# Two-MLP in-projections: 42 matmuls by seven half-depth products where four tiles took 48, with the third token block kept plain

## The chip, the core and the metric

One core of a Trainium2 chip runs the kernel. The metric is device time in microseconds of one execution. The core has five engines that run side by side and meet through semaphores: TensorE (PE, matmuls; its weight loads have a row of their own, PEld), VectorE (DVE), ScalarE (ACT), GpSimd (POOL) and SyncE (SP), whose queue issues nearly all transfers here.

## What is computed

An attention over pooled queries, then a softplus MLP, then a gated MLP behind an RMS normalisation, all in float32:

```python
q_pool = q.reshape(B, H, S // 2, 2, D).mean(axis=3)              # B 2, H 8, S 1152, D 64
scores = scale * np.matmul(q_pool, k.transpose(0, 1, 3, 2))
attn = softmax(scores)                                           # over the 1152 keys
x = (attn @ v) as 1152 tokens x 512
h = x @ moe_w_in                                                 # 512 x 2048
x = softplus(h) @ moe_w_out                                      # 2048 x 512
xn = x / sqrt(mean(x * x) + 1e-6) * rms_g
g, val = xn @ w_gate, xn @ w_val                                 # 512 x 1536 each
out = (g * sigmoid(g) * val) @ w_out                             # 1536 x 512
```

## The kernel before

Every activation lies transposed, features on the 128 partitions and tokens along the columns. The 1152 tokens are three blocks of N = 384 columns. A float32 product is made of three matmuls in the round format: an operand is split into a high half and the rest (hi, lo), and `terms` (lines 643 to 646) adds hi x hi, hi x lo and lo x hi in one PSUM bank.

The attention comes first: 8 pairs of heads (`pb`), each of 5 steps (`x`); in a step `qk` (L476) makes scores, `softmax` takes the maximum on VectorE (L490) and the exponential on ScalarE (L492), `flip` (L511) transposes, `av` (L536) multiplies by v. While it runs, `prep` loads and splits the next pair's operands, `shift` and `split` scale a finished pair and split it into the halves `X[t]` of the token blocks, and `decode` brings the first weight tiles in.

Weights lie in memory as 64-bit numbers. `decode(n)` loads a tile of 128 x 512 into `raw` (L268), scales one word on ScalarE (L316), shifts the other on VectorE (L321), joins them (L324 and L326) and splits the result into hi (copy, L257 or L259) and lo (subtraction, L262). A tile has a place of its own, `slots`.

First MLP: for each block t and each of J1 = 16 tiles j, `m1_h` calls `project` (12 matmuls over KC = 4 chunks of the depth 512), takes the softplus (L666) and splits it (`halve`: L257 or L259, L262); `m1_out` calls `expand` (12 matmuls into the four `out` banks). The loop runs over 48 (t, j), with `m1_h` two ahead. Second MLP: for each block and each of J2 = 12 tiles, `m2_in` projects with the gate and the value tile, takes silu (L773), multiplies (L775), splits; `m2_out` expands. Between them `norm_sum`, `norm_rows`, `norm_turn` and `norm` normalise a block and split it into halves again (L759, then L257, L259, L262).

The program doesn't write down an order for the engines. Each step is entered with the engines that may take it and an estimated duration; `Plan.order` and `Plan.run` lay the steps out by due time and write them out in that order. TensorE's steps keep the order in which they were entered. Which engine takes a copy or a subtraction is thus the planner's choice.

## Time and profile before

| | |
|---|---|
| timed runs | 687.08, 687.18, 687.88 us; median 687.18 |
| span of the profiled execution, first to last instruction | 684.7 us |
| the median above that span | 2.5 us |
| TensorE busy | 675.8 us, 99% of the span |
| VectorE, ScalarE, GpSimd busy | 433.1, 333.3, 112.5 us |
| granted TensorE clock, mean | 0.997 of 2.4 GHz |

The page of the profile gives each engine's busy time, the span in slices, and the chain of work that ended last. The views of the trace give groups of equal instructions with their mean duration, the waits, and the instructions of a stretch in order of time. Busy time of TensorE counts two matmuls that are in flight as one stretch, so that a matmul's own duration is longer than the distance to the next; how fast TensorE goes is read from that distance.

### The profile page before, as it was taken

The page shows a single profiled execution, that of the slowest core. Times are in us where ns is not written, and L with a number is a line of the kernel's source. Part 1 is how long each engine was busy: PE and PEld are TensorE (multiplying, and loading weights), DVE is VectorE, ACT ScalarE, POOL GpSimd, SP SyncE. Part 2 cuts the span into 40 slices and gives each one's busy share as a digit, 9 for nine tenths or more (in the row PEclk, how much of TensorE's full clock was granted, in tenths as well). Part 3 has the DMA queues.
Part 4 walks back from the last instruction along what each step waited for, and adds up shares of the span by engine and source line. Part 5 has one row for each costly group of instructions (what it writes and reads, how often), then busy time and mean ns, then how long its engine had stood idle before and what let it go on. Part 6 is the DMA issues. An engine that isn't in the chain of part 4 may idle for free.

```text
span 684.7 us, 12439 instructions
## 1 busy us (share of the span) xinstructions
PE 675.8 (99%) x5067; PEld 654.4 (96%) x5067; DVE 433.1 (63%) x756; ACT 333.3 (49%) x613; POOL 112.5 (16%) x128
## 2 busy tenths in 40 slices
PE   8999999999999999999999999999999999999997
PEld 7998989898898989999999999999999999999997
DVE  8876787787787779998324468888775412231222
ACT  4887888768888886663212333464531300010001
POOL 0551544426332222000000000011221000000000
PEclk9999999999999999999999999999999999999999
DMA  7543433244321234554000023342540100010001
GB/s 203 170 130 90 127 99 94 74 113 124 101 84 63 81 115 164 187 190 147 0 1 1 32 91 113 134 154 95 183 156 30 47 0 1 1 47 0 1 1 46
DMA packets 20854, 59.77 MB, mean 87 GB/s; under 512 B 3839, under 2 KB 6206, under 8 KB 20798
## 3 DMA queue, kind: packets, MB, share of 16 engines
q1 hardware_dynamic: 20286, 58.63, 27.1%
q8 instruction: 39, 0.64, 0.4%
q10 hardware_dynamic: 512, 0.36, 0.2%
q14 instruction: 17, 0.14, 0.1%
HBM read 56.59 MB, written 2.39 MB: 86 GB/s over the span
## 4 chain that ended last, share of the span: by engine, by line
PE 97%; DVE 1%; DMA 1%; ACT 0%; issue 0%; ACTq 0%; DVEq 0%
PE s L644 16%; PE s L645 16%; PE s L646 16%; PE s L476 12%; PE t L536 11%; PE t L511 10%; PE t L646 5%; PE t L645 5%; PE t L644 5%; PE t L816 1%; DMA kr<-in_kT_dram 1%; ACT pt L257 0%; DVE pt L259 0%; PE t L840 0%; PE s L714 0%; DVE kk L262 0%
## 5 line engine op out<-in xcount | busy, mean ns | idle before, releaser
L644 PE MATMUL s<-x,w 128*128 128x384 f32 x348 | 117.3, 337 | 0.0
L646 PE MATMUL s<-x,w 128*128 128x384 f32 x348 | 116.7, 335 | 0.0
L645 PE MATMUL s<-x,w 128*128 128x384 f32 x348 | 116.7, 335 | 0.0
L490 DVE TENSOR_REDUCE nm<-s 128x1 f32<-128x1152 f32 x72 | 97.7, 1357 | 25.4 <-PE s L476 23.9
L492 ACT ACTIVATE p<-s,nm 128x1152 f32<-128x1152 f32 x72 | 88.3, 1226 | 14.4 <-DVE nm L490 12.9
L773 ACT ACTIVATE g<-s 128x384 f32<-128x384 f32 x36 | 17.7, 492 | 143.0 <-PE s L646 142.9
L257 ACT COPY pt<-t 128x512 f32<-128x512 f32 (+2 forms) x138 | 71.2, 528 | 32.6 <-PE t L511 24.0
L511 PE MATMUL t<-ident,p 128*128 128x128 f32 x576 | 83.5, 278 | 2.5 <-DVE pt L259 1.4
L645 PE MATMUL s<-gl,w 128*128 128x384 f32 x243 | 81.6, 336 | 0.0
L644 PE MATMUL s<-gh,w 128*128 128x384 f32 x243 | 81.6, 336 | 0.0
L646 PE MATMUL s<-gh,w 128*128 128x384 f32 x243 | 81.5, 335 | 0.0
L536 PE MATMUL t<-pt,v 128*64 128x128 f32 (+1 forms) x1440 | 80.1, 265 | 0.0
L511 PEld LDWEIGHTS t<-ident,p 128*128 128x128 f32 x576 | 65.0, 140 | 14.0 <-issue 4.5
L536 PEld LDWEIGHTS t<-pt,v 128*64 128x64 f32 x1440 | 71.3, 137 | 7.2 <-issue 7.0
L644 PEld LDWEIGHTS s<-x,w 128*128 128x128 f32 x348 | 65.4, 188 | 0.2 <-issue 0.2
L645 PEld LDWEIGHTS s<-x,w 128*128 128x128 f32 x348 | 65.4, 188 | 0.0
L646 PEld LDWEIGHTS s<-x,w 128*128 128x128 f32 x348 | 65.4, 188 | 0.0
L262 DVE TENSOR_TENSOR gl<-g,gh 128x384 fp32r<-128x384 f32 x83 | 47.3, 570 | 8.9 <-ACT gh L257 6.8
L316 ACT ACTIVATE t<-raw 128x512 f32<-128x512 f32 x68 | 44.8, 670 | 15.7 <-DVE w L262 13.6
L326 DVE SCALAR_TENSOR_TENSOR t<-t,t 128x512 int32<-128x512 int32 x68 | 47.5, 699 | 1.2
L666 ACT ACTIVATE g<-s 128x384 f32<-128x384 f32 x36 | 17.7, 492 | 62.5 <-PE s L646 58.9
L259 DVE CAST gh<-g 128x384 fp32r<-128x384 f32 x56 | 20.2, 360 | 43.6 <-PE t L646 39.5
(149 smaller groups left out, 1200.9 us busy)
## 6 DMA issues: line engine op xcount, KB each, us to landing
raw<-in_w_dram SPq DMA_DIRECT2D x16, 512.0 KB, 3.7
raw<-in_w1o_dram SPq DMA_DIRECT2D x16, 512.0 KB, 3.4
qr<-in_qT_dram SPq DMA_DIRECT2D x28, 288.0 KB, 4.1
raw<-in_wg_dram SPq DMA_DIRECT2D x12, 512.0 KB, 3.5
raw<-in_wv_dram SPq DMA_DIRECT2D x12, 512.0 KB, 3.8
raw<-in_w2o_dram SPq DMA_DIRECT2D x12, 512.0 KB, 3.5
v<-in_v_dram SPq DMA_DIRECT2D x16, 288.0 KB, 3.3
kr<-in_kT_dram SPq DMA_DIRECT2D x7, 576.0 KB, 4.1
```

The lines of the kernel that those rows point to most:

```text
L257: nc.scalar.copy(out, in_)
L262: engines[e].tensor_tensor(out=out, in0=in0, in1=in1, op=o)
L316: o = op([("ACT", 0.68)], lambda e: nc.scalar.activation(out=t0(), in_=word(1).bitcast(F32), scale=2.0 ** -112, **(dict(func=AF.Prelu, alp ...
L326: op([dve(DM)], lambda e: nc.vector.scalar_tensor_tensor(out=t0().bitcast(I32), in0=t0().bitcast(I32), scalar=3, in1=t1(), op0=ALU.logical ...
L476: nc.tensor.matmul(sc()[:, c, :N], lhsT=q()[:, cut], rhs=k()[:, c * N:(c + 1) * N], start=(i == 0), stop=(i == len(todo) - 1))
L490: u["mx"] = op([dve(S, psum=True)], lambda e: nc.vector.tensor_reduce(out=nm(), in_=sc()[:, :, :N], axis=AX.XY, op=ALU.max, negate=True), ...
L492: o = op([("ACT", 1.42)], lambda e: nc.scalar.activation(out=pr(), in_=sc()[:, :, :N], func=AF.Exp, bias=nm(), accum_out=s["den"]()[:, col ...
L511: nc.tensor.transpose(t()[:, i * P:(i + 1) * P], pr[:, c * P:(c + 1) * P], ident)
L536: nc.tensor.matmul(t()[h * D:h * D + D, :n], lhsT=s["v"][h]()[:, c, :], rhs=rhs, start=(c == 0), stop=(c == CK - 1))
L644: nc.tensor.matmul(out, lhsT=w[:, 0, cols], rhs=hi, start=start, stop=False)
L645: nc.tensor.matmul(out, lhsT=w[:, 0, cols], rhs=lo, start=False, stop=False)
L646: nc.tensor.matmul(out, lhsT=w[:, 1, cols], rhs=hi, start=False, stop=stop)
```

## The change

The in-projections of two weight tiles against two token blocks, four tiles of 12 matmuls, are now made from seven products of half the depth (6 matmuls each: two chunks by three terms). The scheme is Winograd's form of Strassen's: with the tiles' depth halves as rows and the token blocks as columns, four mixtures of the weights (`mix`, lines 414 to 417 of the new kernel) and four differences of the tokens (`Tokens.begin` and `end`: t1 to t4) stand for one product less in eight. In the first MLP tiles 2J and 2J + 1 make a pair and blocks 1 and 2 the columns; in the second MLP the gate and the value tile J make a pair and blocks 0 and 1 the columns. The remaining block (0 in the first, 2 in the second) is projected by plain products (`one_by_one`).

`seven` gives the order p1, p5, p2, p6, p7, p3, p4 on three PSUM banks a, b and f. A result that two tiles share is not added by an instruction of its own: `forward` copies a bank into the next (p1 from a to b, p6 from b to f) or into SBUF (`sp`, p5), and the next product adds into the filled bank with `start` false. The two tiles of the first block leave as they are, the other two are added to `sp` (`added`).

Block 0 of the first MLP is expanded inside the loop of 8 passes; the softplus of blocks 1 and 2 is kept whole (`kept`) and expanded afterwards, 16 tiles each (`first_last`, `step`). The second MLP's loop of 12 passes fills in the last five steps of block 2, the plain tiles of block 2 and the expansions of block 0; blocks 1 and 2 are expanded at the end, 12 tiles each.

`decode` takes two tiles at a time and works in place in the loaded room. The weights' halves, the tokens' halves, the kept tiles and the rooms lie in five areas of SBUF (`AREAS`, in columns of four bytes): `Plan.alloc` gives a place, `free` ends its life, and whoever gets it next waits for all users of the last owner. The attention stays as it is but for the split of its result: `arrived` splits block 0 as it comes, and makes the differences of blocks 1 and 2.

```diff
+AREAS = {"KF": 11330, "KR": 15360, "MR": 8760, "LR": 13632, "LF": 4608}
...
+    def alloc(self, cols, areas, end=0):
+        best = None
+        for rank, name in enumerate(areas.split()):
+            size, region = self.areas[name]
+            mine = [h for h in self.held if h[0] == name]
+            edges = {e for h in mine for e in h[1:3]} | {0, size}
+            for at in sorted(edges if end >= 0 else {e - cols for e in edges}):
...
+                over = [h for h in mine if h[1] < at + cols and at < h[2]]
+                if at < 0 or at + cols > size or any(h[3].live for h in over):
+                    continue
+                key = (rank, end * at) if end else (max([h[4] for h in over], default=0), rank, at)
+                if best is None or key < best[0]:
...
+        for b in self.placed:
+            for o in b.ops:
+                for p in b.prior:
+                    for u in p.users:
+                        o.deps.update(u.ops)
...
+    def halve(hi, lo, x, hp, lp, xp, a, z, at=0):
+        n = z - a
+        i, j = a - at, z - at
+        op([dve(n, True), act(n)], lambda e: copy(e, hi()[:, i:j], x()[:, a:z]), r=[(x, p) for p in xp], w=[(hi, p) for p in hp])
+        op([dve(n), pool(n)], lambda e: tt(e, lo()[:, i:j], x()[:, a:z], hi()[:, i:j], ALU.subtract),
+           r=[(hi, p) for p in hp] + [(x, p) for p in xp], w=[(lo, p) for p in lp])
...
-    def decode(n):
-        src, j = pieces[n]
-        b = view = place(n)
-        weights[src, j] = (b, view)
-        raw = ring("k", "raw", [P, 2 * DM], I32, 2)
...
+    def decode(srcs, combine, phase, fs, rs):
+        b = Halves(rs)
+        s = Halves(rs) if combine else None
+        room = plan.alloc(2 * W, fs)
...
+        cuts = ((0, 1), (1, 2)) if phase == "exp" else ((0, 2),)
...
+            op([dve(n, True)], lambda e, x0=x0, x1=x1: nc.vector.tensor_scalar(
+                out=word(0, x0, x1), in0=word(0, x0, x1), scalar1=29, scalar2=None, op0=ALU.logical_shift_right), w=w0)
...
+            mix(0, (1, 2), (1, 0), ALU.subtract, [first, second])
+            mix(1, (1, 3), (1, 2), ALU.add, [second])
+            mix(2, (1, 3), (0, 0), ALU.add, [second, (room, (0, 0))])
+            mix(3, (1, 1), (0, 2), ALU.subtract, [first])
...
+                op([act(n)], lambda e, w=w, t=t, x0=x0, x1=x1: copy(
+                    e, each(t.hi, x0, x1), word(w, x0, x1).bitcast(F32)), r=rp, w=hp)
+                op([pool(n)] if phase == "exp" else [dve(n), pool(n)], lambda e, w=w, t=t, x0=x0, x1=x1: tt(
+                    e, each(t.lo, x0, x1), word(w, x0, x1).bitcast(F32), each(t.hi, x0, x1), ALU.subtract), r=rp + hp, w=lp)
+        plan.free(room)
...
+        def sub(self, out, x, y, kks):
+            out, x, y = self.of(out), self.of(x), self.of(y)
+            a, z = kks[0] * N, (kks[-1] + 1) * N
+            parts = [(k, i) for k in kks for i in range(2)]
+            op([dve(z - a)], lambda e: tt(e, out()[:, a:z], x()[:, a:z], y()[:, a:z], ALU.subtract),
+               r=[(b, p) for b in (x, y) for p in parts], w=[(out, p) for p in parts])
+        def begin(self, kks):
+            n, m = self.two
+            self.sub("t1", (0, m), (0, n), kks)
+            self.halves("b11", (0, n), kks)
+        def end(self, kks):
+            n, m = self.two
+            self.sub("t2", (1, m), "t1", kks)
+            self.halves("t1", "t1", kks)
+            self.sub("t4", (1, n), "t2", kks)
+            self.halves("b21", (1, n), kks)
+            self.halves("t2", "t2", kks)
+            self.sub("t3", (0, m), (1, m), kks)
+            if 1 in kks:
+                plan.free(self.of((0, m)))
+            self.halves("t3", "t3", kks)
+            self.halves("b22", (1, m), kks)
+            self.halves("t4", "t4", kks)
...
+    def arrived(pb):
+        b, k = divmod(pb, H // 2)
+        if b == 0:
+            X1.split_alone(k)
+        elif k == 1:
+            X1.begin([0, 1])
+        elif k > 1:
+            X1.end([k - 2])
...
-    def project(bank, src, j, x):
-            for k in range(KC):
-                terms(view(), w(), slice(k * P, (k + 1) * P), xh()[:, k, :], xl()[:, k, :], k == 0, k == KC - 1)
...
+    def product(bank, w, x, start, seeded=False, stop=True):
+            out = bank()[:, :N]
+            for k in range(2):
+                for i, (a, b) in enumerate(((w.hi, x.hi), (w.hi, x.lo), (w.lo, x.hi))):
+                    nc.tensor.matmul(out, lhsT=a(k), rhs=b(k), start=start and k + i == 0, stop=stop and k + i == 3,
+                                     skip_group_check=seeded)
+        op([("PE", 6 * MM)], go, r=w.deps + x.deps, w=[(bank, None)])
+    def forward(out, o, bank, sbuf):
+        op([act(N, False), dve(N, psum=True)], lambda e: copy(e, out()[:, :N] if not sbuf else out(), bank()[:, :N]),
+           r=[(bank, None)], w=[(out, o)])
+    def added(out, bank, sp):
+        op([dve(N, psum=True)], lambda e: nc.vector.tensor_tensor(out=out(), in0=sp(), in1=bank()[:, :N], op=ALU.add),
+           r=[(bank, None), (sp, None)], w=[(out, None)])
+    def seven(row, col, X, a, b, f, done):
+        (s0, j0), (s1, j1) = row
+        sp = ring("k", "sp", [P, N])
+        def p1():
+            product(a, plain(s0, j0, 0), X.get("b11"), True)
+            forward(b, None, a, False)
+        def p5():
+            product(f, mixed(s0, j0, 1), X.get("t1"), True)
+            forward(sp, None, f, True)
+        def p2():
+            product(a, plain(s0, j0, 1), X.get("b21"), False, True)
+            done("11", a)
+        def p6():
+            product(b, mixed(s0, j0, 2), X.get("t2"), False, True)
+            forward(f, None, b, False)
+        def p7():
+            product(b, mixed(s0, j0, 0), X.get("t3"), False, True)
+            done("22", b, sp)
+        def p3():
+            product(f, mixed(s0, j0, 3), X.get("b22"), False, True)
+            done("12", f, sp)
+        def p4():
+            product(b, plain(s1, j1, 1), X.get("t4"), False, True)
+            done("21", b)
+        return p1, p5, p2, p6, p7, p3, p4
...
+    def one_by_one(bank, src, j, X):
+        for half in range(2):
+            product(bank, plain(src, j, half), X.single(half), half == 0, stop=half == 1)
...
-    for i in range(n1):
-        t, j = divmod(i, J1)
-        if i + 2 < n1:
-            m1_h(i + 2)
-        m1_out(i)
...
+    n1 = J1 // 2
+    later = {0: [(first_pair, 3), (first_out, 3)], 1: [(first_pair, 4), (first_out, 4)], 2: [(first_out, 5)],
+             3: [(first_pair, 5), (first_out, 6)], 4: [(first_pair, 6)], 5: [(first_pair, 7)], 6: [(first_out, 7)]}
+    for J in range(n1):
+        j = 2 * J
+        p1, p5, p2, p6, p7, p3, p4 = seven((("w1", j), ("w1", j + 1)), None, X1, ab, bb, fb, m1_done(J))
+        expand("w1o", j, kept.pop((0, j)), Y)
+        p1()
+        p5()
+        if J + 1 < n1:
+            m1_alone(j + 2, nb)
+        p2()
+        p6()
+        expand("w1o", j + 1, kept.pop((0, j + 1)), Y)
+        p7()
+        p3()
+        drop("w1", j, 2)
+        if J + 1 < n1:
+            m1_alone(j + 3, nb)
+        if J + 2 == n1:
+            X1.free_alone()
+        p4()
+        drop("w1", j, 0)
+        for make, n in later.get(J, ()):
+            make(n, "soft", FS, RS)
+    X1.free_two()
+    X2 = Tokens(2, (0, 1), FS, RS, RS)
+    evict(Y, 0)
...
+    for j in range(J1):
+        first_last(1, j, X)
+        if j in (0, 6):
+            second_pair(j // 6)
+        if j == 2:
+            norm_sum(0)
+        if j == 5:
+            norm_rows(0, Y[3])
+        if j == 8:
+            norm(0, Y[3])
+        if j == 10:
+            second_out(0)
+    evict(X, 1)
...
+    def step(j):
+        first_last(2, j, Y)
+        if j % 2:
+            drop("w1o", j, 0)
+        if j == 0:
+            norm_sum(1)
+        if j == 5:
+            norm_rows(1, nb)
+        if j == 7:
+            norm(1, nb)
+            X2.begin([0, 1])
+            X2.end([0, 1])
+        if j == 9:
+            second_pair(2)
+        if j == J1 - 1:
+            kept_free()
+            evict(Y, 2)
+            norm_sum(2)
...
+    begin = 11
+    fill = {J: [lambda j=begin + 3 * J + i: step(j) for i in range(3 - J)] for J in range(2)}
+    fill[2] = [lambda: (second_first(0), norm_rows(2, nb)), lambda: second_first(1)]
+    for J in range(3, J2):
+        fill[J] = [lambda j=j, w=w: alone(j, w) for j in {3: (0,), 4: (1, 2), 5: (3, 4)}.get(J, (J - 1,)) for w in range(2)]
+        fill[J].insert(0 if J == 3 else len(fill[J]), lambda j=J - 1: second_first(j))
+    for j in range(begin):
+        step(j)
...
+    for J in range(J2):
+        p1, p5, p2, p6, p7, p3, p4 = seven((("wg", J), ("wv", J)), None, X2, ab, bb, fb, m2_done(J))
+        todo = iter(fill[J])
+        def filler(*counts):
+            if len(fill[J]) in counts:
+                next(todo)()
+        p1()
+        p5()
+        filler(3, 5)
+        p2()
+        filler(5)
+        p6()
+        filler(2, 3, 5)
+        p7()
+        filler(5)
+        p3()
+        drop("wg", J, 2)
+        filler(2, 3, 5)
+        p4()
+        if J == 2:
+            norm(2, nb)
+        for make, n in more.get(J, ()):
+            make(n)
+    X2.free_two()
+    kept_halves("2")
+    for which, bank in enumerate((nb, ab)):
+        alone(J2 - 1, which, bank)
+    second_first(J2 - 1)
+    store(Y, 0)
```

TensorE in the first MLP, one in-projection tile of before (`s_3413` is its bank, `x0` the token block, `w18` the tile):

```order
L644 MATMUL s_3413<-x0_1169,w18_3732 128x384
L645 MATMUL s_3413<-x0_1169,w18_3732 128x384
L646 MATMUL s_3413<-x0_1169,w18_3732 128x384
L644 MATMUL s_3413<-x0_1169,w18_3732 128x384
L645 MATMUL s_3413<-x0_1169,w18_3732 128x384
L646 MATMUL s_3413<-x0_1169,w18_3732 128x384
L644 MATMUL s_3413<-x0_1169,w18_3732 128x384
L645 MATMUL s_3413<-x0_1169,w18_3732 128x384
L646 MATMUL s_3413<-x0_1169,w18_3732 128x384
L644 MATMUL s_3413<-x0_1169,w18_3732 128x384
L645 MATMUL s_3413<-x0_1169,w18_3732 128x384
L646 MATMUL s_3413<-x0_1169,w18_3732 128x384
```

And of the new kernel, the in-projection part of the first half of a pass: p1, p5, one plain tile of block 0, p2, p6 (`s_3452` is bank a, `t_3462` f, `s_3369` b, `s_3316` the plain tile's bank; the areas hold weights and tokens):

```order
L838 MATMUL s_3452<-areaMR_3055,areaKR_954 128x384 x6
L838 MATMUL t_3462<-areaMR_3055,areaKR_954 128x384 x6
L838 MATMUL s_3316<-areaKR_954,areaLR_3448 128x384 x12
L838 MATMUL s_3452<-areaMR_3055,areaKR_954 128x384 x6
L838 MATMUL s_3369<-areaMR_3055,areaKR_954 128x384 x6
```

A tile of 12 rows on one bank became products of 6 on changing banks, with a plain tile of 12 between them.

VectorE at the normalisation of the second block (block 1), before: `x2` is the block, `rs` its row factors, `t0`, `t1` and `raw` a weight tile's decoding, `gl` the lo half of an activation:

```order
L759 SCALAR_TENSOR_TENSOR x2_4766<-x2_4766,rgs_76,rs_5151 128x384
L262 TENSOR_TENSOR w15_3637<-t0_5298,w15_3637 128x512
L262 TENSOR_TENSOR gl_5360<-g_5336,gh_5356 128x384
L324 SCALAR_TENSOR_TENSOR t0_5358<-t0_5358 128x512
L326 SCALAR_TENSOR_TENSOR t0_5358<-t0_5358,t1_5339 128x512
L321 TENSOR_SCALAR t1_5381<-raw_5315 128x512
L324 SCALAR_TENSOR_TENSOR t0_5362<-t0_5362 128x512
L259 COPY x2_5400<-s_3496 128x384
L259 COPY x2_5400<-t_3508 128x384
L326 SCALAR_TENSOR_TENSOR t0_5362<-t0_5362,t1_5381 128x512
L321 TENSOR_SCALAR t1_5408<-raw_5365 128x512
L259 CAST w17_3726<-t0_5362 128x512
```

And in the new kernel: the four row steps (L1024), then the differences and splits for the seven products (768 columns), with the lo halves of kept tiles (384 columns) between them:

```order
L1024 SCALAR_TENSOR_TENSOR areaKF_265<-areaKF_265,rgs_76,s_3316 128x384 x4
L323 TENSOR_TENSOR areaKR_954<-areaKF_265,areaKR_954 128x384
L323 TENSOR_TENSOR areaKF_265<-areaKF_265 128x768
L320 CAST areaMR_3055<-areaKF_265 128x768
L323 TENSOR_TENSOR areaMR_3055<-areaKF_265,areaMR_3055 128x768
L323 TENSOR_TENSOR areaKR_954<-areaKF_265,areaKR_954 128x384
L323 TENSOR_TENSOR areaKF_265<-areaKF_265 128x768
L320 CAST areaMR_3055<-areaKF_265 128x768
L323 TENSOR_TENSOR areaMR_3055<-areaKF_265,areaMR_3055 128x768
L323 TENSOR_TENSOR areaKF_265<-areaKF_265 128x768
L323 TENSOR_TENSOR areaKR_954<-areaKF_265,areaKR_954 128x384
L323 TENSOR_TENSOR areaKF_265<-areaKF_265 128x768
```

The row steps stood apart with weights' work between them; now they stand together, and the operands of the second MLP's first pass follow directly.

## Rows read from the trace of the kernel before

**Rows 1.** The page: busy us (share) and instructions; the chain's shares by engine.

```profile
PE 675.8 (99%) x5067; PEld 654.4 (96%) x5067; DVE 433.1 (63%) x756; ACT 333.3 (49%) x613; POOL 112.5 (16%) x128
PE 97%; DVE 1%; DMA 1%; ACT 0%; issue 0%; ACTq 0%; DVEq 0%
```

**Rows 2.** Stretches: length, then each engine's busy us (instructions), clock, DMA, GB/s.

```profile
core 0: us, PE busy (x) PEld busy (x) DVE busy (x) ACT busy (x) POOL busy (x), PEclk, DMA share, GB/s
0.00:256.50 256.50, 251.11 (x2615) 230.40 (x2616) 197.16 (x299) 201.49 (x357) 90.84 (x110) 0.99 0.39 111
256.50:457.00 200.50, 200.50 (x1160) 200.13 (x1159) 139.89 (x270) 84.48 (x164) 8.08 (x7) 1.00 0.30 101
457.00:681.00 224.00, 224.00 (x1296) 223.83 (x1294) 95.69 (x187) 46.74 (x92) 13.61 (x12) 1.00 0.13 45
...
260.00:280.00 20.00, 20.00 (x116) 19.72 (x115) 18.89 (x33) 13.20 (x26) 2.50 (x2) 1.00 0.53 185
280.00:300.00 20.00, 20.00 (x117) 20.00 (x117) 19.42 (x36) 13.47 (x25) 0.00 (x0) 1.00 0.61 206
```

**Rows 3.** Waits of PE (0 to 257) and of PEld (257 to 684): us, times, longest.

```profile
PE s L476 <- DVE kk L262: 1.5, 2, 1.1
PE t L840 <- POOL ident masks.py:199: 1.4, 1, 1.4
PE t L511 <- DVE pt L259: 1.4, 4, 0.4
PE t L511 <- ACT pt L257: 1.1, 5, 0.2
...
PEld s L645 <- DVE gl L262: 0.3, 1, 0.3
```

**Rows 4.** Timeline of TensorE: start us, us, instruction; these are 60 matmuls apart.

```profile
262.91 0.33 PE L644 MATMUL s<-gh,w 128*128 128x384 f32 x1
...
273.31 0.33 PE L644 MATMUL s<-x,w 128*128 128x384 f32 x1
```

**Rows 5.** The end of the span, in order of time.

```profile
680.88 0.34 PE L646 MATMUL t<-gh,x 128*128 128x384 f32 x1
681.25 0.36 DVE L259 COPY raw<-t 128x192 f32<-128x192 f32 x1 [0.49 <-PE t L646]
...
681.99 0.36 ACTq L792 DMA_DIRECT2D out_dram<-raw  x1
```

**Rows 6.** Groups by shape: line, engine, operation, count | busy us, mean ns.

```profile
L326 DVE SCALAR_TENSOR_TENSOR t<-t,t 128x512 int32<-128x512 int32 x68 | 47.5, 699 | 1.2
L262 DVE TENSOR_TENSOR gl<-g,gh 128x384 fp32r<-128x384 f32 x83 | 47.3, 570 | 8.9 <-ACT gh L257 6.8
L316 ACT ACTIVATE t<-raw 128x512 f32<-128x512 f32 x68 | 44.8, 670 | 15.7 <-DVE w L262 13.6 <-DMA raw<-in_w1o_dram 1.2 <-DMA raw<-in_wv_dram 0.6
L262 DVE TENSOR_TENSOR w<-t,w 128x512 fp32r<-128x512 f32 x50 | 34.6, 694 | 3.8 <-ACT w L257 3.6
L257 ACT CAST w<-t 128x512 fp32r<-128x512 f32 x52 | 32.0, 617 | 7.5 <-DVE t L326 5.9 <-PE t L645 1.4
L321 DVE TENSOR_SCALAR t<-raw 128x512 int32<-128x512 int32 x68 | 30.9, 454 | 1.3
L259 DVE CAST gh<-g 128x384 fp32r<-128x384 f32 x56 | 20.2, 360 | 43.6 <-PE t L646 39.5 <-PE s L745 3.2
L262 POOL TENSOR_TENSOR w<-t,w 128x512 fp32r<-128x512 f32 x15 | 19.7, 1316 | 107.4 <-ACT w L257 102.0 <-DVE w L259 5.3
L775 DVE TENSOR_TENSOR g<-g,s 128x384 f32<-128x384 f32 x18 | 10.0, 555 | 55.3 <-PE s L646 55.2
L759 DVE SCALAR_TENSOR_TENSOR x<-x,rgs,rs 128x384 f32<-128x384 f32 x12 | 6.9, 613 | 0.9 <-ACT rs L257 0.9
L257 ACT COPY t<-s 128x384 f32<-128x384 f32 x6 | 2.9, 481 | 10.2 <-PE s L646 10.2
```

**Rows 7.** Timeline of VectorE and of GpSimd, 444 to 466 us.

```profile
444.08 0.69 DVE L324 SCALAR_TENSOR_TENSOR t<-t 128x512 f32<-128x512 f32 x1
444.69 0.69 DVE L262 TENSOR_TENSOR w<-t,w 128x512 fp32r<-128x512 f32 x1
445.29 0.68 DVE L326 SCALAR_TENSOR_TENSOR t<-t,t 128x512 int32<-128x512 int32 x1
...
456.58 1.13 DVE L321 TENSOR_SCALAR t<-raw 128x512 int32<-128x512 int32 x1
...
455.97 1.46 POOL L262 TENSOR_TENSOR x<-x,x 128x384 fp32r<-128x384 f32 x1
...
464.62 1.02 POOL L262 TENSOR_TENSOR x<-x,x 128x384 fp32r<-128x384 f32 x1
```

**Rows 8.** The page: DMA issues, count, KB each, us to landing.

```profile
raw<-in_w_dram SPq DMA_DIRECT2D x16, 512.0 KB, 3.7
```

More of the change, by code (lines that the diff above doesn't have):

```diff
@@ L681, in go @@
         def go(e):
             for m in range(KC):
-                terms(banks["out"][m][2](), w(), slice(m * P, (m + 1) * P), gh(), gl(), first, last)
-        op([("PE", 12 * MM)], go, r=[(wb, None), (gh, None), (gl, None)], w=[(b, m) for b, m, _ in banks["out"]])
-    def m1_out(i):
-        t, j = divmod(i, J1)
-        expand("w1o", j, gs.pop(i), j == 0, j == J1 - 1)
-        if j == J1 - 1:
-            for m in range(KC):
-                b, part, view = banks["out"][m]
-                op([act(N, False), dve(N, psum=True)], lambda e, m=m, view=view: copy(e, x2[t]()[:, m, :], view()), r=[(b, part)],
-                   w=[(x2[t], m)])
@@ L709, in norm_rows @@
-    def norm_rows(t, acc):
-        b, m, view = spare(0)
+                at = x * DM + m * P
+                wh, wl = b.hi()[:, at:at + P], b.lo()[:, at:at + P]
+                o = out[m]()[:, :N]
+                nc.tensor.matmul(o, lhsT=wh, rhs=gh(), start=first, stop=False)
+                nc.tensor.matmul(o, lhsT=wh, rhs=gl(), start=False, stop=False)
+                nc.tensor.matmul(o, lhsT=wl, rhs=gh(), start=False, stop=last)
+        op([("PE", 12 * MM)], go, r=b.deps(x) + [(gh, None), (gl, None)], w=[(o, None) for o in out])
@@ L860, in body @@
                 prep(pb + 1)
[L861 removed]
+            for make, n in early.get((pb, x), ()):
+                make(n, "exp", "KF", "KR")
             T = turn(pb, x)
@@ L934, in body, with second_last @@
+    X2.free_two()
[4 more added lines that the diff above has]
+    store(Y, 0)
+    def second_last(t, j, out):
+        g = kept.pop((t, j))
+        expand("w2o", j, halved(g, "y"), out)
+        plan.free(g)
+    for j in range(J2):
+        second_last(1, j, X)
+    store(X, 1)
+    for j in range(J2):
+        second_last(2, j, Y)
+    store(Y, "last")
     for which, name in (("soft", "softplus"), ("silu", "silu_and_others")):
```

561 lines of the change are left out of this document (332 added, 229 removed).

## Prediction

> **What bounds the kernel now.** I read the shares by engine and the chain of waits first: TensorE is busy for 675.8 of 684.7 us, and 97% of the chain that ended last is its own work [rows 1]. A busy TensorE can hide waiting, so the next view is the table by stretch [rows 2]: the attention takes 0 to 256.5 us, the first MLP to about 457, the second to 681. In both MLPs TensorE is busy without a gap, at the full granted clock, even from 280 to 300 us, where VectorE is busy for 19.42 of 20 us. In the whole of both MLPs one wait of a weight load is listed, 0.3 us [rows 3]. Third, the pace: two rows of the timeline that are 60 matmuls apart start at 262.91 and 273.31 us [rows 4], so one 128x384 matmul takes 10.40 / 60 = 0.1733 us. Its own row says 0.33 us because two are in flight; the pitch is what counts. The MLPs hold 2448 of them, 2448 x 0.1733 = 424 us, which is the two stretches. So a matmul that is left out of the MLPs is worth 0.1733 us, as long as the other engines keep up.
>
> **What the change takes away.** An in-projection tile was 4 K-chunks x 3 terms = 12 matmuls; there are 16 x 3 of them in the first MLP and 24 x 3 in the second: 576 + 864 = 1440. Now two weight tiles against two token blocks (four tiles, 48 matmuls) are made by seven products of 2 chunks x 3 terms, 42 matmuls. There are 8 such passes in the first MLP and 12 in the second, 840 matmuls; the third token block stays plain, 16 x 12 + 24 x 12 = 480. Together 1320. The out-projections keep their 1008. The order of instructions has these counts, 1320 and 3 x 336, so that the matmuls are fewer is no forecast. Saved: 120 x 0.1733 = **20.8 us**, 8.3 of it in the first MLP and 12.5 in the second. The three normalisations, the table loads and the end (last matmul at 680.88, then a copy in halves and its store [rows 5]) stay as they are.
>
> **What it adds on TensorE's way.** A product adds into a PSUM bank that another engine has filled: p1 is copied from bank a into b, p5 into SBUF, p6 from b into f. Each copy reads a bank that a later product writes. A copy takes 0.48 us on ScalarE or 0.56 on VectorE [rows 6]. Between p6's end and p7 there is an expansion or a plain tile, 12 matmuls, 2.08 us, in nearly all passes; between p1 and p2 there are p5 and mostly another 12, 3.1 us. So these copies cost nothing while ScalarE and VectorE take them within 1.5 us. The cover is short in three places: the last pass of the first MLP and the second and third passes of the second, where only p5 (1.04 us) stands between p1 and p2, and in the first of these only p3 (1.04 us) between p7 and p4. A copy of 0.5 us fits into 1.04 only if its engine is free; behind an instruction of 1024 columns it comes about 0.6 us late. Four places: between 0 and 4 x 0.6 = 2.4 us; I take 0.6.
>
> **The tokens' new operands.** Before, a block's two halves were made from its rows alone, and normalised rows came long ahead of their use (VectorE's old order has one row's step, then a dozen others, then the next). Now p5, p6, p7 and p4 want differences over both blocks. At the start of the second MLP these cannot exist until block 1 is normalised, and TensorE has from that transposition on only three expansions, then p1, p5, an expansion, p2, p6, an expansion, p7, p3, an expansion before p4: 108 matmuls, 18.7 us. VectorE's order there has the four row steps, the differences and the splits for t1, t2, t3, b22 and t4 in a row. With 0.61 for a row step, 0.57 for a 384-column subtraction, 0.94 for 768 (by the slope between the 384 and the 512 rows), 0.55 for a 768 cast and 1.19 for 1024 [rows 6] they sum to 18.5 us up to t4; successive VectorE instructions that don't wait start up to 0.09 us before the listed end of the last (444.08, 444.69 and 445.29 us at 0.69 each [rows 7]), so 16.7 to 18.5 against 18.7. This is the tightest place: between 0 and 4 us are lost; I take 1.0. At the end of the attention the same happens for K-chunk 3 of blocks 1 and 2: 7.3 us of VectorE work (rows of the same kind) against 6.2 us until p2, which needs only part of it, and 14.6 until p4. I take 0.2 there, at most 1.5.
>
> **The side engines' load.** A pair of tiles now also needs four 256-column mixtures and a second split. From the new order, counted and priced by [rows 6]: in the first loop VectorE has 37 subtractions or additions of 384 (0.57), 24 of 256 (0.45), 37 instructions of 1024 (1.19), 13 shifts of 1024 (0.71), 9 copies (0.56) and 6 casts (0.36), 92 us; ScalarE 66; GpSimd 8 splits, 15. TensorE's time there is 8 x 90 matmuls less the 24 that stand ahead, 696 x 0.1733 = 120.6. In the 27 expansions that follow (56.2 us) VectorE has 61 us, of which 12 may run on into the next loop; in the second loop (166.4) VectorE 111, ScalarE 84, GpSimd 44. So VectorE stays under TensorE in each, at about 80% where the first MLP of before ran at 97% for 20 us and lost nothing. Durations that no row shows are the in-place steps on every second word: at worst a shift runs like any other instruction (1.19 for 0.71) and 1024 columns cost two of 512 (1.39 for 1.19), at best as above. That adds 13 x 0.48 + 37 x 0.2 = 14 us to the 92, still below 120.6. I take nothing for it, and leave 2 us in the range.
>
> **The attention.** Nine early tiles become eight, but four of these are split twice and mixed. VectorE: 9 x 1.15 = 10.4 us before, 8 x 1.15 + 8 x 0.45 = 12.8 now; ScalarE 11.6 against 8 x 0.67 + 12 x 0.62 = 12.8; GpSimd 11.8 against 15.8. The differences and splits of the tokens add some 5 us of VectorE. It is busy for 197 of 256.5 us and ScalarE for 201 [rows 2], and TensorE lost 5.4 us there, of which [rows 3] name small waits. Eight more microseconds of side work in 256 give between -0.5 and +3; I take 0.2.
>
> **Sum.** 684.7 - 20.8 + 0.6 + 1.0 + 0.2 + 0.2 = 665.9 for the profiled span. The timed runs lie 2.5 us above it (687.18), so **668.4 us**.
>
> **Rivals.** *VectorE and GpSimd become the bound* between the normalisation and the third pass of the second loop. From the first of the 27 expansions to the plain tile that needs block 2, TensorE has 324 + 210 + 36 matmuls, 98.8 us; VectorE has 89 us of instructions there, GpSimd 22. One row shows that they can exclude each other: a shift of usually 0.43 us took 1.13 from 456.58 while a GpSimd split ran from 455.97 to 457.43, itself 1.46 instead of 1.02 as at 464.62 [rows 7]. If all of GpSimd's time blocked VectorE, 111 - 98.8 = 12 us would go: 668.4 + 12 - 1 = 679; for a third of it, 672. Against it: a third of VectorE's instructions there read PSUM or only one operand, and in the hot stretches of before (GpSimd 2.5 us in 260 to 280 [rows 2]) nothing was lost, though little GpSimd work stood there. The Trainium skill (SBUF — State Buffer, Who interferes with whom) states the stronger form, an exclusive lock held for a whole instruction, for VectorE instructions with two SBUF inputs or in a two-port mode. The trace agrees in that row, and by that rule this rival would be nearer to its 12 us than to a third.
>
> *The attention gives some back* (its side engines delay a transposition's copy in some of the 40 steps): +3 us, 671.
>
> *Slower than before: weights come just in time.* The areas hold little more than two pairs beside the tokens' halves and the out-weights, so a pair's halves are written where the pair two before has just been read. If nothing of its decoding could run ahead, a pair would take 3.7 us of landing [rows 8], 1.08 and 0.71 for the first steps, 2.4 for the next two, 1.8 for the mixtures and 2.2 for the first split, 11.9 us, against 7.3 us from p3's end to the next plain tile: 4.6 us late, for the six pairs of the first loop 28 us, 668.4 + 28 - 2 = 694. It decides from 3.5 us a pair on. Against it: only the last split must wait for the place, 2.2 us of the 7.3; landing and decoding work in another area, which is full of kept tiles only at the loop's end.
>
> **How the numbers follow.** Forecast 0.68, its own range 665 (copies and operands free, attention 0.5 better) to 671. VectorE and GpSimd bound, 672 to 680: 0.16. Attention, 669 to 674: 0.07. Weights late, 690 and more: 0.05. Something that gives more than 20.8 and lost nothing, below 665: 0.04. The range 665 to 676 holds the forecast, the attention and half of the VectorE case, 0.83. A measurement of this kernel tells 0.2%, 1.4 us, from no change: faster 0.94, same 0.01, slower 0.05.
>
> **What would show it.** Right: the pitch stays 0.1733 us, the MLPs hold 2328 matmuls, the stretch of both is some 18 to 20 us shorter, and the waits of TensorE and its weight loads there stay below 3 us in all, most of them on VectorE's splits at the entry of the second MLP. VectorE shows 75 to 85% in the first loop. Wrong: a pitch above 0.175; waits on splits of weights in passes 5 to 7 of the first loop (weights late); a row of waits from the normalisation to the third pass, with VectorE above 95% and GpSimd beside it (the first rival); an attention stretch over 258 us.

## The result, and the profile after

The changed kernel takes 676.36 us (median of 4 runs, 676.11 to 677.46) beside 687.13 us of the kernel before: a ratio of 0.9849, 95% interval 0.9835 to 0.9863. It is faster by 10.8 us where 18.7 were forecast; the time lies 0.4 us above the range of 665 to 676. The profiled execution's span is 675.6 us beside 684.7, where 665.9 was forecast. First the page (busy us, share, instructions; then the chain by engine), which answers to [rows 1]:

```profile
PE 661.1 (98%) x4947; PEld 635.7 (94%) x4947; DVE 493.8 (73%) x762; ACT 380.8 (56%) x626; POOL 170.3 (25%) x158
PE 90%; DVE 6%; issue 1%; DMA 1%; ACT 1%; POOL 0%; ACTq 0%; DVEq 0%
```

TensorE has 120 instructions fewer, as counted, but its part of the chain fell from 97 to 90% and VectorE's rose from 1 to 6%. The waits of TensorE in both MLPs (us in sum, times, longest), where [rows 3] had 0.3 us on a weight load:

```profile
PE t L838 <- DVE areaLF L847: 1.2, 1, 1.2
PE s L838 <- ACT s L318: 1.0, 1, 1.0
PE s L904 <- DVE areaKR L323: 0.7, 4, 0.2
PE s L838 <- DVE areaLF L847: 0.6, 1, 0.6
...
PEld s L904 <- DVE areaKR L323: 2.4, 6, 0.5
```

L838 is a product of the seven, L904 the second matmul of an expansion, which needs the lo half that L323 makes on VectorE; L847 adds sp to a bank. By the timeline the waits stand from 399 to 472 us, in the expansions of blocks 1 and 2 and the first three passes of the second MLP. By the distances between the starts of matmuls they cost 2.8 us in the expansions, 2.4 at the entry of the second MLP (453 to 458 us) and 1.2 in its third pass. What stands ahead of the first of them, in order of time:

```profile
397.04 2.46 POOL L323 TENSOR_TENSOR areaKR<-areaKF,areaKR 128x1024 fp32r<-128x1024 f32 x1 [1.50 <-ACT areaKR L318]
397.51 2.28 DVE L323 TENSOR_TENSOR areaKF<-areaKF 128x256 f32<-128x256 f32 x1
399.71 0.54 DVE L323 TENSOR_TENSOR areaKR<-areaLF,areaKR 128x384 fp32r<-128x384 f32 x1
400.31 0.45 PE L904 MATMUL s<-areaKR 128*128 128x384 f32 x1 [0.22 <-DVE areaKR L323]
```

VectorE's instruction of 256 columns, whose like take 0.42 us, took 2.28 and ended 0.29 us behind GpSimd's split; the lo half that TensorE waited for came next. Two casts at 406.98 and 433.23 us were held up in the same way, 1.81 and 2.37 us where 0.36 is usual, each beside a GpSimd split. Five of the seven late weight loads of the expansions follow such a row. The stretches, as in [rows 2] (length, busy us of each engine):

```profile
258.20:385.00 126.80, 126.80 (x729) 126.80 (x728) 98.37 (x138) 71.99 (x118) 15.94 (x9) 1.00 0.28 100
385.00:457.00 72.00, 70.49 (x398) 67.63 (x397) 60.89 (x102) 29.10 (x43) 13.25 (x7) 1.00 0.21 74
457.00:480.00 23.00, 20.91 (x120) 20.58 (x121) 18.03 (x30) 12.13 (x22) 8.09 (x6) 1.00 0.21 68
```

The first loop (to 385 us) has no gap; VectorE is busy for 98.37 of 126.8 us, 78%. Next the pace. These two matmuls are 287 apart, 24 expansions less one:

```profile
620.17 0.34 PE L903 MATMUL s<-areaMR 128*128 128x384 f32 x1
...
670.34 0.34 PE L905 MATMUL t<-areaKR,areaLR 128*128 128x384 f32 x1
```

50.17 / 287 = 0.1748 us, at the full granted clock, where [rows 4] gave 0.1733. TensorE waits for nobody in this stretch. The kernel before has over its own last 287, from this row to the last matmul at 680.88 [rows 5], 49.82 / 287 = 0.1736 us:

```profile
631.06 0.33 PE L644 MATMUL s<-x,w 128*128 128x384 f32 x1
```

Last the end, in order of time, to be held against [rows 5]:

```profile
670.34 0.34 PE L905 MATMUL t<-areaKR,areaLR 128*128 128x384 f32 x1
...
672.19 0.36 DVE L320 COPY areaLF<-t 128x192 f32<-128x192 f32 x1 [2.50 <-DMA out_dram<-areaLF]
...
672.93 0.36 ACTq L1041 DMA_DIRECT2D out_dram<-areaLF  x1
```

The last copy starts 1.85 us after the start of the last matmul (0.37 in [rows 5]): it waits for a store to leave its buffer. The start of the kernel is 0.97 us later too (first matmul with v at 20.77 us beside 19.80); that is the landing of the first kT load (4.59 us in the chain beside 3.69), which differs from one execution to the next: in the traces of the changed kernel and its variants below this matmul starts between 19.2 and 21.2 us. Between it and the first matmul behind the attention lie 237.50 us, beside 236.78. That one, before and after:

```profile
256.58 0.43 PE L644 MATMUL s<-x,w 128*128 128x384 f32 x1
258.27 0.42 PE L903 MATMUL s<-gh,areaKR 128*128 128x384 f32 x1
```

From there to the last matmul it is 424.30 us before and 412.07 after.

### The profile page after: what moved, and what is told of

The parts are those of the page before. It is cut to its first block, busy times and chain, and to the rows that moved or that the text cites. A ratio compares the mean times of both kernels' runs of the same rounds, so it can differ in the third digit from the quotient of the medians.

```text
span 675.6 us, 12211 instructions
## 1 busy us (share of the span) xinstructions
PE 661.1 (98%) x4947; PEld 635.7 (94%) x4947; DVE 493.8 (73%) x762; ACT 380.8 (56%) x626; POOL 170.3 (25%) x158
## 4 chain that ended last, share of the span: by engine, by line
PE 90%; DVE 6%; issue 1%; DMA 1%; ACT 1%; POOL 0%; ACTq 0%; DVEq 0%
PE s L838 27%; PE s L663 12%; PE t L723 11%; PE t L698 10%; PE t L838 6%; PE s L904 6%; PE s L905 6%; PE s L903 6%; PE t L905 2%; PE t L904 2%; PE t L903 2%; PE t L1065 1%; DVE areaKF L323 1%; DVE areaKR L323 1%; DMA kr<-in_kT_dram 1%
## 5 line engine op out<-in xcount | busy, mean ns | idle before, releaser
L323 POOL TENSOR_TENSOR areaKR<-areaKF,areaKR 128x512 fp32r<-128x512 f32 (+2 forms) x28 | 48.8, 1746 | 148.6 <-ACT areaKR L318 148.5
L838 PE MATMUL s<-areaKR 128*128 128x384 f32 x252 | 61.4, 338 | 0.6 <-DVE areaLF L847 0.6
L318 ACT CAST areaKR<-areaKF 128x1024 fp32r<-128x1024 f32 (+3 forms) x53 | 42.0, 798 | 27.1 <-PE t L905 11.1
L323 POOL TENSOR_TENSOR kk<-kr,kk 64x384 fp32r<-64x384 f32 x42 | 41.2, 1008 | 38.1 <-ACT kk L318 36.7
L320 DVE COPY pt<-t 128x512 f32<-128x512 f32 (+2 forms) x62 | 39.0, 643 | 15.7 <-PE t L698 14.7
L838 PE MATMUL s<-areaKR,areaLR 128*128 128x384 f32 x204 | 49.6, 337 | 0.0
L838 PE MATMUL s<-areaMR,areaKR 128*128 128x384 f32 x218 | 45.8, 338 | 1.0 <-ACT s L318 1.0
L838 PEld LDWEIGHTS s<-areaKR 128*128 128x128 f32 x252 | 45.3, 188 | 1.1 <-DVE areaLF L847 0.9
L323 DVE TENSOR_TENSOR areaKF<-areaKF 128x256 f32<-128x256 f32 (+2 forms) x78 | 41.6, 556 | 0.6
L838 PE MATMUL s<-areaMR,areaLR 128*128 128x384 f32 x190 | 40.2, 338 | 0.0
L838 PEld LDWEIGHTS s<-areaMR,areaKR 128*128 128x128 f32 x218 | 38.6, 188 | 1.3 <-ACT s L318 1.3
L838 PEld LDWEIGHTS s<-areaKR,areaLR 128*128 128x128 f32 x204 | 36.7, 188 | 0.0
L323 POOL TENSOR_TENSOR qs<-qr 128x224 f32<-128x224 f32 (+1 forms) x35 | 21.0, 626 | 61.3 <-DVE qm L599 26.9
```

The costliest lines, as they stand in the source:

```text
L318: nc.scalar.copy(out, in_)
L320: engines[e].tensor_copy(out, in_)
L323: engines[e].tensor_tensor(out=out, in0=in0, in1=in1, op=o)
L838: nc.tensor.matmul(out, lhsT=a(k), rhs=b(k), start=start and k + i == 0, stop=stop and k + i == 3, skip_group_check=seeded)
```

## The experiments

Each is the changed kernel with one edit, if nothing else is said. The times of one kernel scatter by 0.2 to 2.7 us, in part with the landing of the first loads; the traces, cut at the first matmul of the MLPs (the first behind the attention), the last matmul and the end, tell tenths.

**The changed kernel again (e0_repeat).** 

> The changed kernel again, beside which the others of this call are read. What is not of the program but of the one profiled execution should move: the pitch of the matmuls in the last 100 us (174.8 ns in the first profile, 173.4 ns in the kernel before) and the landing of the first kT load (0.9 us later than before). Theory 'it is of the execution': the pitch comes back to 173.4 to 174.0 ns and the span to 672 to 674 us. Theory 'it is of the program (areas instead of separate tiles)': 174.5 to 175.5 ns again and a span of 674.5 to 676 us. Either way the gaps of TensorE between 390 and 475 us stay 6 to 7 us in sum, and the last copy waits 1.5 us for a store.

Measured: 676.14 us, ratio 0.9845 (0.9824 to 0.9867). The pitch of the last 287 matmuls is 174.8 ns again and the waits are the same, to 0.3 us. So the slower pitch belongs to the program. That of single matmuls repeats too: from 485 us on, the intervals between successive starts, from 168 to 185 ns, agree matmul by matmul between the two executions (correlation 0.95).

**The last store (e1_store).**

```
-            ob = (rings["v"] if m % 2 else rings["s"])()
+            ob = (rings["s1"] if t == "last" and m == 3 else rings["v"] if m % 2 else rings["s"])()
```

> The last store of the last token block takes the idle buffer s1 instead of the only buffer v. Theory: 1.5 us of the loss lie behind the last matmul, where VectorE's copy of the last bank waits for the store of the block's second row set to land, because ring v has one buffer; the wait goes, the stretch from the last matmul's start to the end of the span falls from 5.3 to 3.8 us, and the time falls by 1.4 to 1.6 us against e0_repeat. Rival: the last two stores are bound by the queue and the landing of the output, so that the end moves by less than 0.3 us.

```profile
669.25 0.34 PE L905 MATMUL t<-areaKR,areaLR 128*128 128x384 f32 x1
...
669.63 0.36 DVE L320 COPY areaLF<-t 128x192 f32<-128x192 f32 x1 [0.44 <-PE t L905]
```

The wait is gone: 0.38 us from matmul to copy, and 3.9 us to the end of the span instead of 5.26. The time, 676.44 (674.95 to 677.38), doesn't show the 1.4 us that were expected of it; the trace does.

**Four buffers for the halves of kept tiles (e2_halves4).**

```
-            rings[tag] = plan.around(tag + n, N, 2, RS)
+            rings[tag] = plan.around(tag + n, N, 4 if n == "1" else 2, RS)
```

> Four buffers in place of two for the halves of the kept tiles in the first MLP's expansions. Theory A (the split of a kept tile starts too late because its buffer is free only one expansion, 2.1 us, ahead, so that one long VectorE operation is felt): the waits of the expansions' second matmul between 395 and 452 us (3.0 us in sum) fall under 0.6 us; the two waits of the second MLP's first two passes (2.2 us) stay, and the time falls by 2 to 3 us. Theory B (VectorE has no time left between 395 and 460 us): the waits fall by less than 1 us or move to the entry of the second MLP, and the time by less than 1 us.

Measured: 674.19 us (673.37 to 675.97), ratio 0.9815 (0.9790 to 0.9840). The stretch from 385 to 457 us, and all waits of TensorE in the MLPs:

```profile
385.00:457.00 72.00, 72.00 (x419) 71.63 (x418) 60.34 (x102) 32.27 (x49) 13.25 (x7) 1.00 0.26 88
```

```profile
PE s L1021 <- DVE ms L1012: 0.8, 1, 0.8
PE s L838 <- DVE areaLF L847: 0.4, 1, 0.4
PE s L838 <- DVE areaLF L941: 0.2, 1, 0.2
```

Theory A holds, and more than it claimed: VectorE and GpSimd do the same work there as before the edit (60.34 beside 60.89 us, 13.25 beside 13.25), yet no expansion waits, and the entry's two waits, which were to stay, fell from 1.8 to 0.4 us. VectorE had the time; it got the buffers too late. It is still held up beside GpSimd, but with more lead TensorE doesn't feel it:

```profile
396.24 2.67 DVE L323 TENSOR_TENSOR areaKF<-areaKF 128x256 f32<-128x256 f32 x1
```

The wait of 1.0 us for ScalarE in the third pass of the second MLP is gone as well, and a new one of 0.8 us, for the normalisation of block 2 (L1012), stands at the end of that pass. From the first matmul of the MLPs to the last it takes 409.15 us instead of 412.07, although the pitch of the last 287 matmuls rose to 0.1753 us.

**The normalisation two expansions earlier (e3_norm_early).** In `step`, norm_rows(1) and norm(1) moved from j 5 and 7 to 3 and 5.

> The normalisation of block 1 is issued two expansions (4.2 us) earlier. Theory (VectorE is full from the normalisation to the entry of the second MLP, but idle for 1.0 to 1.6 us in each 6 us between 411 and 435 us): the combinations and halves start 4 us earlier, the backlog at the entry of the second MLP is 3 to 4 us shorter, and the waits of the first two passes for the added copies (0.8 and 1.4 us) fall under 0.5 us together: 1.5 to 2.5 us faster than e0_repeat. Rival (VectorE or GpSimd is full earlier too, or the order of VectorE's queue puts weights ahead of the additions at the entry whatever came before): the waits of the entry stay within 0.5 us of 2.2 us, or come back at the expansions.

```profile
PE s L1000 <- DVE ms L323: 1.7, 1, 1.7
PE s L838 <- ACT s L318: 1.3, 1, 1.3
PE s L904 <- DVE areaKR L323: 0.2, 1, 0.2
```

676.34 us: no gain. The entry's waits on L847 are gone, as the theory said, but TensorE now waits 1.7 us for the sum of squares ahead of the normalisation. The wait was moved, not removed.

**Operands at byte 0 or 32 of 64 (e4_pad, e5_before_mixed).** e4_pad: `"LF": 4608` becomes 4616. e5_before_mixed, on the kernel before: gl is `[P, N + 8]`, read from column 8; the tiles behind it begin 64 bytes later.

> The changed kernel with area LF eight columns longer, so that area LR behind it begins 32 bytes later; every engine's instructions stay in the same order. In the kernel before all matmuls of the MLPs read moving operands that begin at byte 32 of 64, and both halves of a weight at the same byte of 64; there the matmuls follow each other in 173.5 ns. In the changed kernel operands begin at byte 0 (KR, MR, gh, gl) or 32 (LR) of 64, and a product often mixes them: 175.0 ns, and 173.4 ns in those expansions where hi and lo have the same byte. Theory (mixing the two bytes within a product costs time): with the pad all of them begin at byte 0, the pitch in the last 180 us comes back to 173.4 to 173.8 ns, and with some 2330 matmuls by 1.0 to 1.5 ns the span falls by 2.3 to 3.5 us against e0_repeat; the waits for VectorE and ScalarE between 395 and 475 us stay at 6 us. Rival (the pitch comes from something else, such as one shared area or byte 0 instead of 32): it stays at 174.7 to 175.3 ns and the time within 0.7 us.

> The kernel before, with the tile gl eight columns wider and read from column 8 on: of its two buffers the first now begins at byte 0 of 64 and the second at byte 32 as gh does; the order of every engine's instructions is the same. Theory (mixing bytes of 64 costs): in the expansions every second one (gh at 32, gl at 0) takes 175 to 176 ns a matmul and the others and the plain products stay at 173.5 ns; 504 matmuls by 1.5 to 2 ns make 0.8 to 1.0 us, which the time hardly shows. Rival (the areas themselves): 173.5 ns in both.

The theory fell on e4_pad: with all operands at byte 0 of 64 the pitch did not improve. The two matmuls 287 apart:

```profile
619.50 0.35 PE L903 MATMUL s<-areaMR 128*128 128x384 f32 x1
...
669.77 0.34 PE L905 MATMUL t<-areaKR,areaLR 128*128 128x384 f32 x1
```

50.27 / 287 = 0.1752 us; time 677.56 (676.55 to 678.36). But e5_before_mixed, one execution, with not one instruction moved, has a span of 687.7 us beside 684.7 of the kernel before:

```profile
633.40 0.33 PE L644 MATMUL s<-x,w 128*128 128x384 f32 x1
...
683.80 0.34 PE L646 MATMUL t<-gh,x 128*128 128x384 f32 x1
```

50.40 / 287 = 0.1756 us, against 0.1736 over the same 287 matmuls of the kernel before. It slowed plain products as well, which don't read gl: those with weights that the 64 bytes had shifted took 530 ns for three matmuls, those with weights that stayed 521. So addresses change the pitch, but not by the byte of 64 alone. The places follow from what each program allocates: in the changed kernel areas KR and MR begin at byte 256 of 512 and LR at 352, in e4_pad LR at 384. Sorted by the distance of the weights' start from the moving operand's, in 512 bytes, the four traces at hand (before, after, e4_pad, e5_before_mixed) fall apart: where hi and lo and the next weights are alike, 0 or +96 gives 520 to 526 ns for three matmuls in the mean, and -96, 128 or 160 gives 528 to 530; where hi and lo differ it is mostly 524 to 529.

**All operands at the same byte of 512 (e8_same512).**

```
-... "LR": 13632, "LF": 4608}
+... "LR": 13568, "LF": 4712}
```

> The changed kernel with area LR 64 columns shorter and LF 104 columns longer, so that every operand of the MLPs' matmuls begins at the same byte of 512 (256, but for 24 matmuls of the attention's end); every engine's instructions stay in the same order. The runs so far, three matmuls of a product or expansion added up: 520 to 521 ns in the kernel before, where the moving operands begin at byte 480 of 512 and the weights at 480 or 64; 530 ns there with the weights moved to byte 128; 522 ns in the padded kernel where all begin at 256, and 527 to 529 ns where weights and moving operand are 128 apart. Theory (the distance of weights and moving operand, taken in 512 bytes, sets the pitch): 521 to 523 ns for three, a pitch of 173.6 to 174.3 ns in the last 180 us, and with 2330 matmuls a span 1.6 to 3.2 us shorter than the changed kernel's. Rival (the place in the whole of SBUF counts, not the distance in 512 bytes): the pitch stays over 174.7 ns.

```profile
257.25 0.42 PE L903 MATMUL s<-gh,areaKR 128*128 128x384 f32 x1
...
616.62 0.33 PE L903 MATMUL s<-areaMR 128*128 128x384 f32 x1
...
666.37 0.34 PE L905 MATMUL t<-areaKR,areaLR 128*128 128x384 f32 x1
```

49.75 / 287 = 0.1733 us, the pitch of [rows 4] and a little under that of the kernel before in this stretch (0.1736), with every instruction in its old order. From the first matmul of the MLPs to the last it takes 409.12 us instead of 412.07: 2.95 us. Time 673.53 (673.07 to 673.87), ratio 0.9813 (0.9800 to 0.9827).

**One order on ScalarE (e7_order).** In the third pass of the second MLP ScalarE copied p5's bank to sp before p1's bank to b, and p2 waited. The edit gives p5's copy an `after` on p1's copy.

> In the changed kernel the copy of bank f to sp, where it is on the same engine, may not start ahead of the copy of bank a to bank b. Theory (the wait of 1.0 us at 470 us, in the third pass of the second MLP, comes of the order on ScalarE, which waits for the later product's bank before it copies the earlier one): this wait goes, and the order elsewhere stays nearly as it was: 0.6 to 1.0 us faster by the trace, hardly seen in the time. Rival (ScalarE and VectorE are both full there, and the copy is late in any order): a wait of 0.7 us or more remains in that pass.

```profile
...
PE s L838 <- DVE s L320: 0.4, 1, 0.4
```

The wait fell from 1.0 to 0.4 us (the copy is VectorE's now), and the MLPs from 412.07 to 411.52; 675.64 us (675.46 to 675.70). The other waits are as they were.

**The edits together (e6_best, e9_best2, e10_best3).** e6_best: e1_store, e2_halves4 and e4_pad. e9_best2: e8_same512's areas in place of e4_pad's. e10_best3: e7_order's edit besides.

> The changed kernel with three edits together: the idle buffer s1 for the last store, four buffers for the halves of the kept tiles in the first MLP, and area LF eight columns longer. If the three losses are separate: 1.3 us from the end, 3.5 to 4.5 us of waits of TensorE between 395 and 475 us, 2.5 to 3.5 us from the pitch: a span of 665.0 to 667.5 us beside 673.9 (the median of the changed kernel's spans), and a time of 667 to 669.5 us. If the pitch is of another cause, 669.5 to 671 us.

> The buffer s1 for the last store, four buffers for the halves of the kept tiles, and all operands at the same byte of 512. Theory: the waits are those of e6_best (1.5 us), the tail 3.9 us, and the pitch 173.6 to 174.3 ns in place of 175.3: a span of 666 to 668 us and a time of 668 to 670 us. Rival as in e8_same512: 670 us and 672 us as e6_best.

> As e9_best2, with the copy of bank f to sp not ahead of the copy of bank a to bank b on one engine. In e7_order this edit took the wait in the third pass of the second MLP from 1.0 to 0.4 us; with four buffers for the halves that wait is not there, so nothing of it is left to gain: within 0.5 us of e9_best2 by the spans, if the new order makes no wait elsewhere.

e6_best has a span of 670.3 us, in the case "pitch of another cause", which is right; its time of 672.20 lies over that range. e9_best2 took 668.45 (667.47 to 670.21), within what was expected (its span, 665.7, is 0.3 us under), ratio 0.9746 (0.9731 to 0.9761). Its first and last matmul of the MLPs:

```profile
256.77 0.42 PE L903 MATMUL s<-gh,areaKR 128*128 128x384 f32 x1
...
661.83 0.34 PE L905 MATMUL t<-areaLR,areaKR 128*128 128x384 f32 x1
```

405.06 us against 409.12 in e8_same512, at the same pitch: the four buffers are worth 4.1 us where no change of the pitch hides a part. e10_best3 took **666.22 us** (665.86 to 666.71), ratio 0.9708 (0.9694 to 0.9721): the expectation that nothing was left for the last edit was wrong by 1.6 us of the MLPs, since the new order also took a wait of 0.9 us for a normalisation. Its waits, first and last matmul of the MLPs, and last copy:

```profile
PE s L838 <- DVE s L320: 0.2, 1, 0.2
PE t L838 <- DVE areaLF L847: 0.2, 1, 0.2
```

```profile
257.15 0.42 PE L905 MATMUL s<-gh,areaKR 128*128 128x384 f32 x1
...
660.60 0.34 PE L907 MATMUL t<-areaLR,areaKR 128*128 128x384 f32 x1
...
660.98 0.36 DVE L320 COPY areaLF<-t 128x192 f32<-128x192 f32 x1 [0.43 <-PE t L907]
```

403.45 us from the first matmul of the MLPs to the last; the kernel before took 680.88 - 256.58 = 424.30. The difference is 20.85 us, and 120 x 0.1733 is 20.8. That they agree so closely is in part luck: 1.0 us of waits is left (at 450 and 463 us), and about as much is won because the matmuls follow each other a little faster than before (0.1733 against 0.1736 in the last 287).

## Why the forecast missed

In the profiled span 675.6 - (684.7 - 20.8) = 11.7 us of the gain are missing, of which the forecast had allowed 2.0. The runs divide them:

| part | us | from |
|---|---|---|
| waits of TensorE in the MLPs | 5.6 | 409.12 (e8_same512) less 403.5, which is 424.30 less 20.8 |
| pitch | 2.95 | 412.07 less 409.12 |
| end of the span | 1.4 | 5.26 less 3.82 |
| attention | 0.7 | 237.50 less 236.78 |
| first load, of this execution | 1.0 | 20.77 less 19.80 |

- **What the change takes away: right.** 120 matmuls at 0.1733 us, 20.8 us, are there once the losses are removed (e10_best3). The sum that all matmuls of the MLPs, 2448 x 0.1733 = 424 us, are the two stretches came out by luck: 24 of them stand ahead of 256.5 us, and gaps of the kernel before, mostly at its normalisations, with a mean pitch a little over 0.1733, make up for these.
- **"I take nothing for it": wrong, about 3 us.** This step, the load of the side engines, is the first that failed. It held VectorE's 61 us against 56.2 of TensorE in the 27 expansions and let the rest run on. But a total doesn't say when a piece is ready. With two buffers a split cannot start before the expansion two earlier has ended, one expansion (2.1 us) ahead of its use, and in between VectorE not only works at weights in pieces of 1.22 us, it is also held up beside GpSimd's splits, for 1.5 to 2.0 us at a time (the rows at 397 us). Four buffers took these waits away (2.4 us of them listed on weight loads) at the same load and with hold-ups of the same size. That the lead was too short is thus shown; no run took GpSimd's splits away, so what the hold-ups alone cost stays open. The forecast should have listed, for each operand of TensorE, the lead its buffers allow beside the longest run of VectorE's instructions in between, hold-ups included.
- **The entry of the second MLP, +1.0 (0 to 4): within its bounds, 1.8 us by the listed waits and 2.4 by the starts, but by another way.** It was not the differences for p4 that came late: p4, and p5 of the next pass, waited 0.63 and 1.25 us for L847's additions, which stood behind the weights of pair 2 in VectorE's order. GpSimd's rows come first:

```profile
450.10 1.16 POOL L323 TENSOR_TENSOR areaKR<-areaKF,areaKR 128x384 fp32r<-128x384 f32 x1 [14.72 <-ACT areaKR L318]
454.81 1.53 POOL L323 TENSOR_TENSOR areaKR<-areaKF,areaKR 128x384 fp32r<-128x384 f32 x1 [3.54 <-ACT areaKR L318]
...
450.46 1.22 DVE L323 TENSOR_TENSOR areaKR<-areaKF,areaKR 128x384 fp32r<-128x384 f32 x1
451.60 1.54 DVE L323 TENSOR_TENSOR areaLF<-areaLF 128x256 f32<-128x256 f32 x4
453.06 0.95 DVE L323 TENSOR_TENSOR areaKR<-areaKF,areaKR 128x768 fp32r<-128x768 f32 x1
453.94 0.55 DVE L847 TENSOR_TENSOR areaLF<-sp,s 128x384 f32<-128x384 f32 x1
454.40 1.22 DVE L323 TENSOR_TENSOR areaLR<-areaLF,areaKR 128x1024 fp32r<-128x1024 f32 x1
455.53 1.89 DVE L323 TENSOR_TENSOR areaLR<-areaLF,areaLR 128x1024 fp32r<-128x1024 f32 x1
457.53 0.55 DVE L847 TENSOR_TENSOR areaLF<-sp,t 128x384 f32<-128x384 f32 x1
```

  Two VectorE rows here were held up by 0.67 us each beside a GpSimd split: 1.22 us for 384 columns (usually 0.56), and 1.89 for 1024 (usually 1.22). In e2_halves4 the last of them takes 1.22, with no GpSimd split beside it, and the waits are 0.4.
- **Copies with short cover, +0.6 (0 to 2.4): right in size, not in cause.** One of the four places cost 1.0 us (1.2 by the starts), the third pass of the second MLP. The copy was not late behind an instruction of 1024 columns; ScalarE had p5's copy ahead of it (e7_order).
- **"The pitch stays 0.1733 us": wrong, 2.95 us.** It was not a term at all. The change puts operands into areas whose bases are 96 bytes apart in 512, and with equal bases the old pace is back (e8_same512). The prediction named a pitch above 0.175 as a sign of error; at 0.1748 the pitch stayed just under it while it cost 2.95 us, so the sign was set too high.
- **The end ("stay as they are") [rows 5]: wrong, 1.4 us.** The new kernel gives ring v one buffer (its line 1222); the second and fourth stores of a block share it. The line was read for the MLP's loop, not for the last store.
- **Attention, +0.2 (-0.5 to 3): within its bounds, +0.7.** Set against the kernel before, TensorE falls back by 0.4, 0.2 and 0.3 us at about 81, 94 and 125 us; what makes these delays was not tried. The stretch ended at 258.3 us, over the 258 that the prediction named as a sign, by the late first load.
- **The rival of VectorE and GpSimd** gave the right place, and the measured time lies in its range (672 to 680). That it lies there is in part luck: without the pitch and the end, which are no part of it, the time would be 672.0, its lower end. Its mechanism was at work, but not as a bound. By the usual durations of equal instructions, VectorE's rows between 385 and 480 us are 7.9 us longer in all where GpSimd runs beside them. The Trainium skill (SBUF — State Buffer, Who interferes with whom) states a lock held for a whole instruction between VectorE with two SBUF inputs and GpSimd's reads of SBUF; the rows at 397, 450 and 455 us agree, as each held instruction ends behind GpSimd's. What falls is that the two engines had no time left: VectorE is busy for 60.89 of 72 us from 385 to 457, hold-ups included, 85% where the prediction asked for more than 95. In e10_best3 it has the same 60.89 us there, 5.8 of them by hold-ups, and TensorE is busy for 71.79 of the 72. Nor does the price follow from its own sum: a third of GpSimd's 22 us on top of VectorE's 89 is 96.3, under TensorE's 98.8, and would cost nothing.
- **The slower rival, weights just in time,** did not come: no wait of TensorE is put down to a weight's split.

## To carry to other kernels

When work is taken from the engine that sets the pace, cost the others by deadlines, not by totals: how far ahead of its use a buffer lets each operand be made, what stands before it in its engine's order, and how long one of those instructions may be held up by another engine (2 us here). When tiles are packed into areas of one's own, compare the pitch before and after; here the same byte of 512 for the bases of all operands of the matmuls brought it back. And read every ring that shrinks at each place that uses it, the last store too.

## What the runs showed of the hardware

The pitch of matmuls depends on where weights and moving operand lie within SBUF's partitions. With the order of instructions unchanged, 64 bytes of shift took the kernel before from 0.1736 to 0.1756 us a matmul (one execution), and a change of two area sizes took the changed kernel from 0.1748 back to 0.1733. Equal bytes of 512 are shown to be good, distances of 128 and 160 to be slower by 2 to 3 ns a matmul; why, and whether 512 is the true period, stays open.

In the changed kernel's trace behind 258 us, no VectorE instruction with all its operands in SBUF that starts while a GpSimd split runs ends before the split does: 2.28 us instead of 0.42 at 397.51, 2.37 instead of 0.36 at 433.23, 1.89 instead of 1.22 at 455.53. Those that read PSUM take their usual time: an addition of L847 at 465.83 took 0.55 us beside a split of 2.46 from 465.58.
